# Long convolution and soft mixture of experts on one core: combine weights gathered per batch in SBUF instead of written per tile

## The chip, the core and the metric

One core of a Trainium2 chip runs the whole program in one launch. The metric is the device time in microseconds. The engines named below are TensorE (PE, with its weight loads PEld), VectorE (DVE), ScalarE (ACT), GpSimd (POOL) and SyncE (SP), which here only issues DMAs.

## The reference

A causal convolution of each of 8 sequences (5696 positions, 128 channels) with one filter of full length, then a soft mixture of experts over all 45568 tokens:

```python
Xf = np.fft.rfft(x, n=2*S, axis=1); Hf = np.fft.rfft(h, n=2*S, axis=0)
x = np.fft.irfft(Xf * Hf[None], n=2*S, axis=1)[:, :S, :].reshape(B*S, D)
logits = x @ phi                            # 45568 x 32 slots (8 experts x 4)
d = softmax(logits, over all tokens)        # dispatch weights
slot_input = d.T @ x                        # 32 x 128
slot_out[e] = relu(slot_input[e] @ w1[e]) @ w2[e]
c = softmax(logits, over the 32 slots)      # combine weights
out = c @ slot_out
```

The output needs `slot_out`, which needs every token. The combine weights `c` (45568 x 32 numbers) therefore have to be kept from the time a token tile is made until the last stage.

## The kernel before

**Stages.** The convolution is two transform stages forward (`first_stage`, then `stage_b1` with the product in frequency), and two back (`stage_b2`, then `stage_c1`). Between them stand two internal DRAM tensors, `f` and `z`. The rest works on 32 token tiles, T = 0 to 31, four for each of 8 batches (`NQ = 4`). For a tile, `load_pair` brings 1.4 MB of `z` (five DMAs, of 64, 8, 8, 8 and 2 rows of 16 KB), and then:

- `stage_c1` multiplies back to tokens: 16 matmuls, and folds on DVE, ACT and POOL into the buffer `y`. It runs `stage_c4` of an earlier tile between its two halves.
- `stage_c2` transposes `y` (PE, copies `yt` on ACT), `stage_c3` makes logits `lt`, `column_max` keeps the running maximum (DVE).
- `stage_c4` transposes the logits into `L` (tokens x slots), takes `exp` into `dt` (ACT), clears the last rows of `dt` (POOL, line 439), and subtracts the row maximum of `L` (DVE, POOL line 447). `stage_c5` transposes `dt` into `d` (PE line 454). `softmax` finishes `L`, which then holds the combine weights.
- `dispatch` adds `d.T @ y` to the accumulator `acc`.
- `stage_c6` transposes `L` so that slots lie on partitions (4 transposes, line 502).

**Where the combine weights go.** The last stage reads one table, `cT`, of 128 x 8 x 89 x 16 (slots and quarters on partitions; batch, row, column). It takes 45.6 KB of each partition, and there is room for it only when the transform tables have been freed, near the end. Until then `stage_c6` copies its PSUM bank in one ACT instruction into a staging tile `cst` (line 512) and stores 180 KB of it to the DRAM tensor `c_t` (line 513). That is done for T = 0 to 24. From T = 25 on `cT` exists, and `stage_c6` writes its four quarters straight into it (line 507; `place` gives the reversed or forward rows and columns of each quarter). In the last loop `fetch_c` and `load_c` bring the stored tiles back, a batch at a time (720 KB, line 518) into two buffers `cl`; `placed_c` and `place_all` copy them into `cT`, two copies on POOL and two on ACT for each batch (line 524), and then fetch again.

**Order.** The program gives every engine its instructions in the order in which the code is written; nothing moves them later. The main loop runs steps t = 0 to 80, two steps to a tile, with the order of the work in a step given by the strings `ORDER_E` and `ORDER_O` (line 577). All DMAs but four at the start are issued by SP, in program order. They share 8 completion semaphores in turn, so that each DMA waits until the eighth one before it has landed.

**The end.** The main loop ends at t = 80 (lines 625 to 641) with T = 26 as `V`. Then the tables are freed, `cT` is allocated (line 667), and a last loop (lines 699 to 734) runs V = 27 to 31. Its order for V = 28 and later is: `stage_c2(V)`, `dispatch(V-1)`, `stage_c6(V-2)`, `stage_c3(V)`, `column_max(V)`, `placed_c`, `stage_c1(V+2)` with `stage_c4(V)` inside it, `placed_c`, `stage_c5(V)`, `softmax(V)`, and for V = 28 and 29 half of the load of `w2s`. `stage_c1(30)` is so in the iteration V = 28, and `stage_c1(31)` in V = 29. The data of tile 30 are loaded in iteration 27, after `stage_c1(28)` has read the buffer `zd`, and those of tile 31 after `stage_c1(29)` has read `zc`. After the loop come the experts (lines 741 to 797) and the output matmuls with `cT` (lines 812 to 839), which write 23 MB.

Of the kernel before, what the change touches and what calls it, by code (L numbers as in the profile page):

```python
# [10 lines left out]
F32 = mybir.dt.float32  # L11
AF = mybir.ActivationFunctionType
# [65 lines left out]
def kernel(  # L78
# [24 lines left out]
    nc = tc.nc  # L103
    P = 128
    B, S, D = x.shape
# [4 lines left out]
    N1, N2 = 90, 64  # L110
    R1, HALF, NP = S // N2, N2 // 2, N1 // 2
    CH = 4
    NJ = HALF // CH
# [16 lines left out]
        for n, t in zip(("s1", "i1", "w", "v", "turn"), transform_tables(S, N1, N2, CH, X0))]  # L130
    fd = [nc.dram_tensor(f"f_{g}", (NP, 2, N2, 2, D), F32, kind="Internal").ap() for g in range(B + 1)]
    zd = [nc.dram_tensor(f"z_{b}", (NP, 2 * N2, 2, D), F32, kind="Internal").ap() for b in range(B)]
    cd = nc.dram_tensor("c_t", (P, B * NQ, Q, 2, MH), F32, kind="Internal").ap()

    const = ctx.enter_context(tc.tile_pool(name="const", bufs=1))
    ident = const.tile([P, P], F32, name="ident")
# [347 lines left out]
                                           scalar=scales.pop(T)[:, 0:1], in1=ap_[:, 0:D + 1],  # L484
                                           op0=AL.mult, op1=AL.add)

    kept, tail = [], {}

    def place(T, n, k):

        b, j = 2 * T // NJ, 2 * T % NJ
        v, f = divmod(k, 2)
        rows = slice(MH, R1) if v else slice(MH - 1, None, -1)
        e_ = 2 * NJ - 1 - j
        cols = slice(e_, e_ - 2 * n, -1) if f else slice(j, j + 2 * n)
        return tail["cT"][:, b, rows, cols].rearrange("p r (n h) -> p r n h", h=2)

    def stage_c6(T):
        L = Ls.pop(T)
        p = bank()  # L500
        for k in range(Q):
            nc.tensor.transpose(p[:, k * TR:(k + 1) * TR],
                                L[0:TR, k, :, :].rearrange("p i s -> p (i s)"), ident[0:TR, 0:TR])
        pv = of_tokens(p)
        if tail:
            for k in range(Q):
                nc.scalar.activation(place(T, 1, k)[:, :, 0, :],
                                     pv[:, k, :, 0:MH - k // 2].rearrange("p h r -> p r h"), AF.Copy)
            return
        kept.append(T)  # L510
        st = cpool.tile([P, Q, 2, MH], F32, name="cst", tag="cst", bufs=1)
        nc.scalar.activation(st[:, :, :, :], pv, AF.Copy)
        nc.sync.dma_start(out=cd[:, T, :, :, :].rearrange("p k h r -> p (k h r)"),
                          in_=st[:, :, :, :].rearrange("p k h r -> p (k h r)"))

    def load_c(T, n):
        st = tail["pool"].tile([P, NQ, Q, 2, MH], F32, name="cl", tag="cl")
        nc.sync.dma_start(out=st[:, 0:n, :, :, :].rearrange("p n k h r -> p (n k h r)"),
                          in_=cd[:, T:T + n, :, :, :].rearrange("p n k h r -> p (n k h r)"))
        return st  # L520

    def place_all(T, n, st):
        for k in range(Q):
            (nc.gpsimd.tensor_copy if k < 2 else nc.scalar.copy)(
                out=place(T, n, k),
                in_=st[:, 0:n, k, :, 0:MH - k // 2].rearrange("p n h r -> p r n h"))

    def join_quarters():

# [49 lines left out]
    for t in range(last_front + 1):  # L579
        us = list(units(t))  # L580

        def pair(lag):
            T, half = divmod(t - LAG_C - lag, 2)
            return T if half == 0 and 0 <= T < NT else None

        def prefetch(last):
            nonlocal loaded
            while loaded < len(queue) and queue[loaded][1] <= last:
                load_g(queue[loaded][0])
                loaded += 1  # L590

        def slot_b():
            fresh = bool(us)
            if fresh:
                u = us.pop(0)
                stage_b1(u, t < LAG_C or t >= NA)
                wait_b2.append(u)
            if len(wait_b2) > fresh:
                stage_b2(wait_b2.pop(0))

        T, U = pair(0), pair(2)
        after = []
        work_ = {
            "z": lambda: load_pair(pair(-1)) if pair(-1) is not None else None,
            "x": lambda: load_x(t + XAHEAD) if t < NA else None,
            "p": lambda: prefetch(t + 1) if t % NJ else None,
            "P": lambda: prefetch(t + 2),
            "q": lambda: prefetch(t + 1),
            "X": lambda: first_low(t) if t < NA else None,
            "Y": lambda: first_high(t) if t < NA and t % 2 else None,  # L610
            "f": lambda: [fold(t + 1, comp) for comp in range(2)] if t < NA else None,
            "d": lambda: dispatch(pair(3)) if pair(3) is not None else None,
            "b": lambda: slot_b(),
            "1": lambda: after.append(stage_c1(T, lambda: stage_c4(U) if U is not None else None))
            if T is not None else stage_c4(U) if U is not None else None,
            "w": lambda: [a_() for a_ in after],
            "2": lambda: stage_c2(pair(1)) if pair(1) is not None else None,
            "6": lambda: stage_c6(pair(5)) if pair(5) is not None else None,
            "5": lambda: stage_c5(U) if U is not None else None,
            "3": lambda: stage_c3(pair(1)) if pair(1) is not None else None,  # L620
            "m": lambda: column_max(pair(1)) if pair(1) is not None else None,
            "s": lambda: softmax(U) if U is not None else None,
            "g": lambda: prefetch(t + 1) if t % NJ == 0 else None,
        }
        if t == last_front:
            if pair(-1) is not None:
                load_pair(pair(-1))
            assert T is None and U is None
            if pair(3) is not None:
                dispatch(pair(3))  # L630
            slot_b()
            slot_b()
            slot_b()
            stage_c2(pair(1))
            slot_b()
            assert not us and not wait_b2
            V = pair(1)
            stage_c6(V - 2)
            stage_c3(V)
            column_max(V)  # L640
            break
        for c_ in (ORDER_E if t % 2 else ORDER_O):
            work_[c_]()
        assert not us
        if t == NA:
            lead.close()
            wts = inner.enter_context(tc.tile_pool(name="wts", bufs=1, side="right"))
            w1s = wts.tile([P, E, F], F32, name="w1s")
        if NA < t <= NA + E:
            nc.sync.dma_start(out=w1s[:, t - NA - 1, :], in_=moe_w1[t - NA - 1])  # L650
# [14 lines left out]
    load_pair(V + 2)  # L665
    nc.sync.dma_start(out=w1s[:, E - 1, :], in_=moe_w1[E - 1])
    tail["cT"] = last.tile([P, B, R1, 2 * NJ], F32, name="cT")
    w2s = last.tile([P, E, NFC, D], F32, name="w2s")
    tail["rep4"] = rep4 = last.tile([P, Q, NSL], F32, name="rep4")
    tail["pool"] = cload.enter_context(tc.tile_pool(name="cload", bufs=2))  # L670
    y_ = tail["pool"].tile([P, Q * CH, D + 1], F32, name="y2", tag="y2", bufs=1)

    after = stage_c1(T, lambda: stage_c4(V))
# [6 lines left out]
        nc.gpsimd.tensor_copy(out=rep4[r, :, :],  # L680
                              in_=ident[r, r].unsqueeze(1).broadcast_to([NSL, Q, NSL]))
    load_pair(T + 2)
    landed = []

    def fetch_c():
        if kept:
            n = min(NQ, len(kept))
            landed.append((kept[0], n, load_c(kept[0], n)))
            del kept[0:n]

    def placed_c():
        if landed:
            place_all(*landed.pop(0))
            fetch_c()

    fetch_c()
    fetch_c()
    assert (B - 1) * NQ == T + 1
    for V in range(T, NT):
        if V > T:  # L700
            stage_c2(V)
        dispatch(V - 1)
        stage_c6(V - 2)
        if V == T:
            stage_c2(V)
        stage_c3(V)
        column_max(V)
        if V > T:
            placed_c()
        N = T + 1 if V == T else V + 2  # L710
        after = None
        if N < NT:
            after = stage_c1(N, lambda: stage_c4(V))
            load_pair(N + 2)
        else:
            stage_c4(V)
        if after:
            after()
        if V > T:
            placed_c()  # L720
        stage_c5(V)
        if V == NT - 1:
            join_quarters()
            dispatch(V)
        softmax(V)
        if V == T:
            ybufs.insert(0, y_)
            stage_c1(T + 2, lambda: None)()
            load_pair(T + 4)
        else:  # L730
            for i in range(4 * (V - T - 1), min(4 * (V - T), E), 2):
                nc.sync.dma_start(
                    out=w2s[:, i:i + 2, :, :],
                    in_=moe_w2[i:i + 2].rearrange("e (p c) d -> p e c d", p=P))
    stage_c6(NT - 2)
    assert list(Ls) == [NT - 1] and not (ys or ds or prods or gs or zs or xs or folded or wait_b2
                or kept or landed)


    cload.close()  # L740
# [128 lines left out]
```

## Time and profile before

| | |
|---|---|
| device time, median of 3 runs | 871.62 us (869.36 to 871.84) |
| profiled execution, device time | 869.17 us |
| span of its instructions | 867.4 us |
| mean granted TensorE clock | 0.954 |
| PE busy, share of the span | 89% |
| DVE, ACT, POOL busy | 71%, 51%, 47% |
| moved by DMA | 272.46 MB, mean 314 GB/s |

Times inside the run are microseconds from the first instruction. The stages that matter here are: the main loop in its steady state (about 230 to 630 us, some 20 us for a tile), its end (630 to 722), the last loop (722 to 785), the experts (785 to 802) and the output (802 to 867). A wait is charged to what released it last; idle time of an engine matters only where something on the chain to the end waits for it.

### The profile page before, as it was taken

The page shows a single profiled execution, that of the slowest core. Times are in us where ns is not written, and L with a number is a line of the kernel's source. Part 1 is how long each engine was busy: PE and PEld are TensorE (multiplying, and loading weights), DVE is VectorE, ACT ScalarE, POOL GpSimd, SP SyncE. Part 2 cuts the span into 40 slices and gives each one's busy share as a digit, 9 for nine tenths or more (in the row PEclk, how much of TensorE's full clock was granted, in tenths as well). Part 3 has the DMA queues.
Part 4 walks back from the last instruction along what each step waited for, and adds up shares of the span by engine and source line. Part 5 has one row for each costly group of instructions (what it writes and reads, how often), then busy time and mean ns, then how long its engine had stood idle before and what let it go on. Part 6 is the DMA issues. An engine that isn't in the chain of part 4 may idle for free.

```text
span 867.4 us, 20489 instructions
## 1 busy us (share of the span) xinstructions
PE 770.7 (89%) x7796; PEld 376.2 (43%) x7796; DVE 619.2 (71%) x928; ACT 441.6 (51%) x904; POOL 403.7 (47%) x385
## 2 busy tenths in 40 slices
PE   5888888888999999999999999999988879977893
PEld 1122333234444444444444444444444444444882
DVE  3059967667777878877888788877789995953552
ACT  2433344344555565556566556655544445773541
POOL 4453433245565555656555655556434432671000
PEclk9999999999999999999999999999999898989865
DMA  9899899999999999999999999999998986580898
GB/s 294 272 296 310 296 333 342 332 332 334 339 315 321 340 324 329 347 329 345 338 339 337 338 338 339 346 327 343 320 314 283 320 301 247 219 305 2 335 405 341
DMA packets 156109, 272.46 MB, mean 314 GB/s; under 512 B 12183, under 2 KB 113687, under 8 KB 152870
## 3 DMA queue, kind: packets, MB, share of 16 engines
q1 hardware_dynamic: 155435, 270.85, 90.2%
q8 instruction: 62, 1.02, 0.5%
q10 hardware_dynamic: 576, 0.31, 0.1%
q14 instruction: 36, 0.29, 0.1%
HBM read 142.81 MB, written 128.21 MB: 312 GB/s over the span
## 4 chain that ended last, share of the span: by engine, by line
PE 60%; DMA 15%; DVE 11%; SPq 3%; issue 2%; POOL 1%; ACT 1%; DVEq 0%; ACTq 0%
PE bank L217 14%; PE bank L365 13%; PE bank L309 7%; PE bt L267 7%; PE bank L393 6%; DMA zc<-z 6%; DMA out_dram<-o 3%; PE bank L478 3%; DVE yf L294 2%; DVE p L285 2%; DVE bt L285 2%; SPq L346 2%; DMA gt<-f 2%; PE op L822 2%; PE bank L402 2%
## 5 line engine op out<-in xcount | busy, mean ns | idle before, releaser
L206 POOL TENSOR_TENSOR x<-xc 128x512 f32<-128x512 f32 x144 | 180.0, 1274 | 229.5 <-PE bank L217 208.6
L217 PE MATMUL bank<-x,s 128*32 128x512 f32 (+1 forms) x1152 | 227.7, 613 | 16.0 <-DMA xc<-in_h_dram 8.1
L315 ACT ACTIVATE zst<-bank 128x512 f32<-128x512 f32 (+1 forms) x184 | 98.6, 586 | 190.9 <-PE bank L309 173.9
L220 ACT ACTIVATE fst<-bank 128x512 f32<-128x512 f32 x216 | 127.4, 598 | 109.5 <-PE bank L217 93.5
L285 DVE TENSOR_TENSOR p<-bt,Hi 128x1024 f32<-128x1024 f32 x96 | 111.4, 1160 | 33.7 <-PE bt L267 32.8
L309 PE MATMUL bank<-yf,vt 64*64 64x256 f32 x1440 | 103.1, 392 | 27.5 <-DVE yf L294 27.5
L365 PE MATMUL bank<-zc,i 128*64 128x512 f32 x480 | 115.8, 604 | 12.1 <-DMA zc<-z 8.2
L217 PEld LDWEIGHTS bank<-x,s 128*32 128x32 f32 (+1 forms) x1152 | 56.1, 124 | 155.5 <-issue 76.2
L294 DVE TENSOR_TENSOR yf<-bt,p 128x512 f32<-128x512 f32 x192 | 119.4, 663 | 3.3
L267 PE MATMUL bt<-gt,wt 64*64 64x256 f32 x1620 | 113.7, 388 | 5.8 <-DVE Hi L289 2.4
L285 DVE TENSOR_TENSOR bt<-bt,Hr 128x1024 f32<-128x1024 f32 x96 | 113.0, 1177 | 0.0
L267 PEld LDWEIGHTS bt<-gt,wt 64*64 64x64 f32 x1620 | 54.0, 132 | 80.6 <-issue 36.7
L309 PEld LDWEIGHTS bank<-yf,vt 64*64 64x64 f32 x1440 | 57.2, 136 | 58.9 <-issue 27.8
L384 POOL TENSOR_TENSOR y<-y,op 128x512 f32<-128x512 f32 x64 | 77.9, 1217 | 8.3 <-DVE op L370 5.2
L370 DVE TENSOR_TENSOR y<-bank,y 128x512 f32<-128x512 f32 x32 | 22.1, 691 | 72.8 <-PE bank L365 72.6
L393 PE MATMUL bank<-ident,y 109*128 109x109 f32 x512 | 64.3, 278 | 0.7 <-DVE y L384 0.7
L384 POOL TENSOR_TENSOR y<-y,om 128x512 f32<-128x512 f32 x54 | 64.0, 1185 | 2.1
L365 PEld LDWEIGHTS bank<-zc,i 128*64 128x64 f32 x480 | 30.5, 136 | 74.8 <-issue 47.1
L393 PEld LDWEIGHTS bank<-ident,y 109*128 109x128 f32 x512 | 54.3, 151 | 16.7 <-issue 11.1
L395 ACT ACTIVATE yt<-bank 128x360 f32<-128x360 f32 x128 | 51.4, 492 | 3.1 <-PE bank L393 3.1
L439 POOL MEMSET dt<- 64x8 f32 x32 | 3.4, 106 | 104.8 <-issue 70.7
L822 PE MATMUL op<-so,cT 32*128 32x128 f32 x704 | 45.6, 368 | 4.7 <-ACT o L831 4.3
(97 smaller groups left out, 824.6 us busy)
## 6 DMA issues: line engine op xcount, KB each, us to landing
gt<-f SPq DMA_DIRECT2D x99, 512.0 KB
z<-zst SPq DMA_DIRECT2D x88, 512.0 KB
f<-fst SPq DMA_DIRECT2D x144, 240.0 KB
zc<-z SPq DMA_DIRECT2D x30, 1024.0 KB
xc<-in_x_dram SPq DMA_DIRECT2D x64, 320.0 KB
f<-fst SPq DMA_DIRECT2D x144, 120.0 KB
out_dram<-o SPq DMA_DIRECT2D x16, 1024.0 KB
zc<-z SPq DMA_DIRECT2D x90, 128.0 KB
```

What stands on the lines that cost most here:

```text
L206: nc.gpsimd.tensor_tensor(out=y_[:, :, :], in0=t_[:, 0, :, :], in1=t_[:, 1, ::-1, :], op=AL.subtract if comp else AL.add)
L217: nc.tensor.matmul(p[o * width:(o + 1) * width, :], s1[:, comp + G, k], folded[(c, comp)][:, :, :].rearrange("p n d -> p (n d)"), start=Tr ...
L220: nc.scalar.activation(st[:, :, G, :], p[:, :].rearrange("p (n d) -> p n d", d=D), AF.Copy)
L267: nc.tensor.matmul(bt[q * HP:(q + 1) * HP, a, o, :], wt[r, 2 * i + q, :], t_[r, 2 * o + q, :, :].rearrange("p c d -> p (c d)"), start=True ...
L285: nc.vector.tensor_tensor(out=p_, in0=pv, in1=h_, op=AL.mult)
L294: eng.tensor_tensor(out=y_[r, 0:k, c, :], in0=pv[:, :, c, :], in1=pi[r, 0:k, 1 - c, :], op=op_)
L309: nc.tensor.matmul(bz[q][a * HP:(a + 1) * HP, o * 2 * D:(o + 1) * 2 * D], vt[r, i, a, :], y_[r, a * m + o, :, :].rearrange("p c d -> p (c ...
L315: nc.scalar.activation(st[:, 0:m, q, :], bz[q][:, 0:m * 2 * D].rearrange("p (o x) -> p o x", o=m), AF.Copy)
L365: nc.tensor.matmul(p[h_ * HP:(h_ + 1) * HP, :], i1[0:kr, tab, :], t_[0:kr, h_, o, :, q, :], start=True, stop=True)
L384: eng.tensor_tensor(out=part_, in0=part(v, 0), in1=o_[:, :, :], op=sign)
L393: nc.tensor.transpose(p[:, i * TR:(i + 1) * TR], ys[T][0:TR, k * CH + i, 0:D], ident[0:TR, 0:TR])
L822: nc.tensor.matmul(pq[q][:, k * D:(k + 1) * D], cT[rows, b, r0:r0 + RW, :] if k < n else cL[rows, :, :], so4[rows, :], start=True, stop=True)
```

## The change

A tile `cbatch` in SBUF (128 x 89 x 16, 5.7 KB of each partition) has the layout that one batch has in `cT`. `stage_c6` now always writes its four quarters with four ACT copies: into `cbatch` while `cT` doesn't exist, into `cT` after that. After the fourth tile of a batch, `cbatch` is stored with one DMA of 712 KB, six times in all (batches 0 to 5). `stage_c6(24)`, the first tile of batch 6, moves from before `stage_c3(26)` to after the allocation of `cT`, and so writes to `cT`. In the last loop there is no fetching and placing any more: behind `load_pair(T + 2)`, which is tile 29, six DMAs load batches 0 to 5 from DRAM straight into `cT`. The buffers `cl` and the functions `load_c`, `place_all`, `fetch_c` and `placed_c` are gone.

```diff
-    cd = nc.dram_tensor("c_t", (P, B * NQ, Q, 2, MH), F32, kind="Internal").ap()
+    cd = nc.dram_tensor("c_t", (B - 1, P, R1, N2 // 4), F32, kind="Internal").ap()
...
-    kept, tail = [], {}
-    def place(T, n, k):
+    tail = {}
+    cbatch = ypool.tile([P, R1, 2 * NJ], F32, name="cbatch")
+    def place(T, k):
...
-        cols = slice(e_, e_ - 2 * n, -1) if f else slice(j, j + 2 * n)
-        return tail["cT"][:, b, rows, cols].rearrange("p r (n h) -> p r n h", h=2)
+        cols = slice(e_, e_ - 2, -1) if f else slice(j, j + 2)
+        home = tail["cT"][:, b, :, :] if tail else cbatch
+        return home[:, rows, cols]
...
-        if tail:
-            for k in range(Q):
-                nc.scalar.activation(place(T, 1, k)[:, :, 0, :],
-                                     pv[:, k, :, 0:MH - k // 2].rearrange("p h r -> p r h"), AF.Copy)
-            return
-        kept.append(T)
-        st = cpool.tile([P, Q, 2, MH], F32, name="cst", tag="cst", bufs=1)
-        nc.scalar.activation(st[:, :, :, :], pv, AF.Copy)
-        nc.sync.dma_start(out=cd[:, T, :, :, :].rearrange("p k h r -> p (k h r)"),
-                          in_=st[:, :, :, :].rearrange("p k h r -> p (k h r)"))
-    def load_c(T, n):
...
-    def place_all(T, n, st):
         for k in range(Q):
-            (nc.gpsimd.tensor_copy if k < 2 else nc.scalar.copy)(
-                out=place(T, n, k),
-                in_=st[:, 0:n, k, :, 0:MH - k // 2].rearrange("p n h r -> p r n h"))
+            nc.scalar.activation(place(T, k),
+                                 pv[:, k, :, 0:MH - k // 2].rearrange("p h r -> p r h"), AF.Copy)
+        b, last_of = divmod(T, NQ)
+        if not tail and last_of == NQ - 1:
+            nc.sync.dma_start(out=cd[b].rearrange("p r j -> p (r j)"),
+                              in_=cbatch[:, :, :].rearrange("p r j -> p (r j)"))
...
             V = pair(1)
-            stage_c6(V - 2)
+            assert (V - 2) % NQ == 0
             stage_c3(V)
...
     tail["cT"] = last.tile([P, B, R1, 2 * NJ], F32, name="cT")
+    stage_c6(V - 2)
...
     load_pair(T + 2)
-    landed = []
...
-    fetch_c()
-    fetch_c()
+    for b in range(B - 2):
+        nc.sync.dma_start(out=tail["cT"][:, b, :, :].rearrange("p r j -> p (r j)"),
+                          in_=cd[b].rearrange("p r j -> p (r j)"))
...
-        if V > T:
-            placed_c()
...
-        if V > T:
-            placed_c()
```

More of the change, by code (lines that the diff above doesn't have):

```diff
@@ L504, in stage_c6 @@
         pv = of_tokens(p)
-        if tail:
-            for k in range(Q):
-                nc.scalar.activation(place(T, 1, k)[:, :, 0, :],
-                                     pv[:, k, :, 0:MH - k // 2].rearrange("p h r -> p r h"), AF.Copy)
-            return
-        kept.append(T)
-        st = cpool.tile([P, Q, 2, MH], F32, name="cst", tag="cst", bufs=1)
-        nc.scalar.activation(st[:, :, :, :], pv, AF.Copy)
-        nc.sync.dma_start(out=cd[:, T, :, :, :].rearrange("p k h r -> p (k h r)"),
-                          in_=st[:, :, :, :].rearrange("p k h r -> p (k h r)"))
-    def load_c(T, n):
[L517 to L520, printed above, removed]
-    def place_all(T, n, st):
-        for k in range(Q):
-            (nc.gpsimd.tensor_copy if k < 2 else nc.scalar.copy)(
-                out=place(T, n, k),
-                in_=st[:, 0:n, k, :, 0:MH - k // 2].rearrange("p n h r -> p r n h"))
+        for k in range(Q):
+            nc.scalar.activation(place(T, k),
[4 more added lines that the diff above has]
+                              in_=cbatch[:, :, :].rearrange("p r j -> p (r j)"))
     def join_quarters():
@@ L667 @@
     tail["cT"] = last.tile([P, B, R1, 2 * NJ], F32, name="cT")
+    stage_c6(V - 2)
     w2s = last.tile([P, E, NFC, D], F32, name="w2s")
     tail["rep4"] = rep4 = last.tile([P, Q, NSL], F32, name="rep4")
-    tail["pool"] = cload.enter_context(tc.tile_pool(name="cload", bufs=2))
+    tail["pool"] = cload.enter_context(tc.tile_pool(name="cload", bufs=1))
     y_ = tail["pool"].tile([P, Q * CH, D + 1], F32, name="y2", tag="y2", bufs=1)
@@ L682 @@
     load_pair(T + 2)
-    landed = []
[L685 to L693, printed above, removed]
-            fetch_c()
-    fetch_c()
-    fetch_c()
+    for b in range(B - 2):
+        nc.sync.dma_start(out=tail["cT"][:, b, :, :].rearrange("p r j -> p (r j)"),
+                          in_=cd[b].rearrange("p r j -> p (r j)"))
     assert (B - 1) * NQ == T + 1
@@ L735 @@
     stage_c6(NT - 2)
-    assert list(Ls) == [NT - 1] and not (ys or ds or prods or gs or zs or xs or folded or wait_b2
-                or kept or landed)
+    assert list(Ls) == [NT - 1] and not (ys or ds or prods or gs or zs or xs or folded or wait_b2)
     cload.close()
```

## The prediction

> **What bounds the kernel now.** I read the page first, then stretches, then the last loop on PE, POOL and SP in order of time. The stretches (columns: length; busy us of PE, PEld, DVE, ACT, POOL; clock; DMA share; GB/s):
>
> ```profile
> 228.00:630.00 402.00, 395.08 (x4056) 183.78 (x4054) 318.53 (x493) 235.20 (x487) 229.53 (x213) 1.00 0.97 334
> 746.00:765.00 19.00, 16.81 (x136) 8.45 (x134) 18.42 (x30) 14.61 (x34) 15.70 (x16) 1.00 0.51 176
> 765.00:785.00 20.00, 12.07 (x121) 8.49 (x121) 8.86 (x20) 14.06 (x36) 11.62 (x16) 0.83 0.66 258
> ```
>
> In the main loop PE idles 7 us of 402 and the DMA engines are 97% busy: both bind, and ACT (59%) and POOL (57%) have room. In the last loop nothing is full. POOL and ACT are busy there with the copies into `cT`; the group rows and the longest PE waits from 715 to 803 us:
>
> ```profile
> L512 ACT ACTIVATE cst<-bank 128x360 f32<-128x360 f32 x25 | 13.1, 522 | 0.3 <-PE bank L502 0.3
> L524 POOL COPY cT<-cl 128x360 f32<-128x360 f32 (+1 forms) x14 | 11.7, 868 | 2.5 <-DMA cl<-c_t 2.5
> L524 ACT COPY cT<-cl 128x352 f32<-128x352 f32 (+1 forms) x14 | 10.5, 799 | 3.6 <-DMA cl<-c_t 3.6
> L507 ACT ACTIVATE cT<-bank 128x90 f32<-128x90 f32 (+1 forms) x28 | 4.6, 266 | 5.9 <-PE bank L502 5.9
> PE bank L454 <- POOL dt L439: 6.6, 4, 3.8
> ```
>
> PE waits for the POOL memset of `dt`. The chain shows what holds it in V = 30: a `cl` load, and copies behind it.
>
> ```profile
> 760.74 1.69 POOL cT L524 x2
> 762.43 0.02 issue
> 762.45 8.72 DMA cl<-c_t
> ...
> 772.11 0.84 POOL cT L524
> ```
>
> Next, what SP issues before `stage_c1(30)`, and the PE row of that stage:
>
> ```profile
> 728.32 3.68 SPq L346 DMA_DIRECT2D zc<-z  x5
> 732.05 0.89 SPq L518 DMA_DIRECT2D cl<-c_t  x2
> 738.69 3.15 SPq L346 DMA_DIRECT2D zd<-z  x5
> 742.86 3.12 SPq L346 DMA_DIRECT2D zc<-z  x5
> 747.01 1.94 PE L365 MATMUL bank<-zd,i 96*64 96x512 f32 x8
> 757.76 1.94 PE L365 MATMUL bank<-zc,i 128*64 128x512 f32 x8
> ```
>
> The landing times are in the trace's records of the DMA semaphores (the last update before the semaphore is used again):
>
> ```
> load                 first issue   last piece landed   read by PE from
> tile 29 (zc)         728.32        738.39              739.17
> cl, batch 0          732.05        740.20
> cl, batch 1          732.49        741.97
> tile 30 (zd)         738.69        746.90              747.01
> tile 31 (zc)         742.86        752.27              757.76
> ```
>
> Tile 30 lands 0.11 us before PE reads it, and directly behind the two `cl` loads. That is the place to watch.
>
> **What the Trainium skill says.** "DMA: Bandwidth & Descriptors", section "Queues, rings and completion order": on each DMA engine descriptors are consumed in ring order, so loads issued ahead on the same queue go first. The landings agree: `cl` 0, `cl` 1, tile 30, one behind the other. "TensorE: Matmul & The Clock Gate", section "Part 1: The HAM clock gate", says that after about 3.4 us of idling PE runs at half clock until it has been busy for such a window. The trace agrees: PE idles from 770.35 to 774.11, and the 16 matmuls of line 393 then take 3.11 us instead of 1.66.
>
> **The change, part by part.** Times are for the profiled span of 867.4 us (device 869.17); the median is 2.45 us above that run, and I add the difference found to the median.
>
> 1. *Main loop, ACT.* 24 tiles have four copies of 0.266 us (row L507) in place of one of 0.522 us: +0.54 us of ACT for a tile of 20 us, in the gap between the last `yt` copy and `stage_b2`. PE does 2.9 us of `dispatch`, `stage_b1` and `stage_b2` before ACT or the PSUM bank is needed again. Cost 0; uncovered it would be 13 us.
>
> 2. *Main loop, DMA.* 24 stores of 180 KB become 6 of 712 KB, nearly the same bytes (4.4 MB). At 334 GB/s a store takes 0.55 us, the big one 2.2. SP is 8 to 10 us behind the compute here, and `zc` lands only 0.1 to 1.2 us before it is read in most tiles, so this isn't free: three tiles of a batch gain up to 0.55 us where they wait now, and one has a burst of 1.6 us net. Slack at the loads behind the first five bursts (tiles 7, 11, 15, 19, 23) is 0.09, 0.09, 0.34, 0.65, 0.35 us. Bounds: +6.3 us if each burst stalls by 1.6 less its slack and nothing is regained; -2.5 if the lighter tiles take back the waits at tiles 5, 6, 10, 21, 22 and the bursts are absorbed. The work of the queue over a batch is unchanged, so I take 0.
>
> 3. *Wait for `cbatch`.* The first tile of the next batch must wait until the store has been read out. The single stores land 6.3 to 8.8 us after issue, and the next copy comes 2.7 to 7 us after that; 1.6 us more still fits. Cost 0. Uncovered, `zst` and `lt` would queue behind it on ACT, and PE behind their banks.
>
> 4. *`stage_c6(24)` moves.* Its four transposes (0.59 us) stood in the shadow of the last `yt` copy and now stand ahead of `stage_c1(27)`: +0.6 us. In step 6 that disappears in a longer wait.
>
> 5. *Copies gone from the last loop.* 14 POOL and 14 ACT copies, 22.2 us busy, and the waits for `cl`. Without them I rebuild the iterations from PE rows. A full one with `stage_c1`: 4.4 us for the stage with `stage_c4` inside, 0.65 for `stage_c5`, 1.65 for line 393, 1.1 for line 478, 0.6 for 502, 0.8 for 402: 9.1 us from one `stage_c1` to the next (now 10.75). From `stage_c1(31)` to the last line 454 (784.20 now): 5.0 to `stage_c2(30)`, then twice 7.05 with the wait for lt, L, `dt` and its memset, and 0.55 for the transposes: 19.65 us (now 26.4). Gain 1.6 + 6.8 = 8.4 us, if the data are there.
>
> 6. *Six loads ahead of tile 30.* They stand behind tile 29 and before tiles 30 and 31 in the queue, where two stood. Their semaphores come free between 731.4 and 737.1, so all six are in the queue before tile 30 is issued at 738.7. The two `cl` loads took 1.81 and 1.77 us of it; four more take 7.0. Tile 30 lands at 746.9 + 7.0 = 753.9, tile 31 at 759.3. PE arrives at `stage_c1(30)` at 747.6 and waits 6.3 us. That isn't all: a window of 3.4 us is idle, so the clock halves. It stays so for 3.0 to 6.4 us of work, 4.7 in the middle, which loses 2.35 us. The wait holds everything: `stage_c4(28)` is inside `stage_c1(30)`, and ACT, DVE and POOL have their next work from there.
>
> Sum: 753.9 + 2.35 + 9.1 + 19.65 = 785.0 against 784.20: +0.8 us. In V = 30 and 31 PE then idles 2.25 us within 2.9 us twice, and idle gaps of 1.8 to 2.7 us in the trace (634.76, 670.13) were followed by a half-clock window, up to 1.7 us each: I add 1.5. Together +2.3 us. Experts and output (784.9 to 867) keep their length: `w2s` lands at about 769 instead of 779.5, and is needed at 797.
>
> **Forecast.** 871.6 + 2.3 = 873.9 us: the copies go, and the wait that they hid behind takes their place. Chance 0.62. Its own range: 870 to 878.
>
> **Rival, faster.** The queue lets tile 30 through in time, because the loads are quicker or start earlier than I think. Then 747.6 + 9.1 + 19.65 = 776.4, -7.8 us, with perhaps 1 lost to the clock: about 864.5. It decides where tile 30 lands before some 751.5 (784.2 less 28.75, less the 3.9 for the clock). For it: DMA idles from 755.5 to 760 now, so there is room in the queue overall, and 8.4 us of gain are real. Against it: the order on SP, and the rate of 1.77 us a load that the same bytes already show at this place. Chance 0.18.
>
> **Rival, much slower.** The bursts in the main loop find no slack: +6.3 us from part 2, and +2.3: 880. For it: DMA at 97% and slacks of 0.09 us. Against it: the tiles between bursts get lighter by the same sum. Chance 0.20.
>
> **How the numbers follow.** A difference of about 0.3% (2.6 us) is what can be told from none here. The forecast, at +2.3 with some 2.2 either way, gives slower 0.28, same 0.33, faster 0.01. The faster rival gives 0.15 and same 0.03; the slower one 0.20. Sums: faster 0.16, same 0.36, slower 0.48. The range leaves out the faster rival's centre and the upper end of the slower one: 868.5 to 879.
>
> **What would show it.** Right: PE idle for 5 to 7 us before line 365 on `zd` in V = 28, released by the DMA of tile 30; a half-clock window from about 753; no wait over 2 us for the memset afterwards; some 785 at the last line 454. In the main loop: ACT without waits at `cbatch`, PE idle still 5 to 10 us of 402. Wrong: tile 30 landed by 750 (faster), or PE idle of 1 us or more behind each batch's store (slower), or ACT waiting for the store of `cbatch`.

## The result and the profile after

| | before | after |
|---|---|---|
| device time, median of 20 runs each | 872.04 us | 875.87 us |
| profiled execution: span, mean clock | 867.4 us, 0.954 | 875.6 us, 0.94 |

The ratio is 1.005, 95% interval 1.0032 to 1.0067: slower by 3.8 us in the medians, where 2.3 was forecast. The stretches of the changed kernel (columns as in the prediction: length; busy us of PE, PEld, DVE, ACT, POOL; clock; DMA share; GB/s):

```profile
228.00:630.00 402.00, 396.66 (x4076) 184.26 (x4076) 320.20 (x496) 240.51 (x551) 230.77 (x215) 1.00 0.97 335
746.00:765.00 19.00, 14.58 (x96) 7.48 (x92) 12.27 (x18) 6.59 (x18) 7.13 (x7) 0.64 0.91 368
765.00:785.00 20.00, 17.38 (x182) 11.41 (x175) 12.89 (x29) 11.48 (x31) 8.16 (x9) 0.83 0.02 9
```

The main loop is what it was: PE idles 5.3 us of 402 (6.9 before). From 746 on DMA is now 91% busy (51% before) and then empty, POOL's 15.7 us have become 7.1, and the clock is 0.64 where it was 1.00. The order in which SP issues (start, length, what) shows how that comes about:

```profile
729.11 3.14 SPq L346 DMA_DIRECT2D zc<-z  x5
732.29 3.71 SPq L672 DMA_DIRECT2D cT<-c_t  x6
740.09 3.14 SPq L346 DMA_DIRECT2D zd<-z  x5
```

PE waits for the last of these. Its rows in order of time (start, time to the end of the group, what; in brackets the idle time before it and what ended it):

```profile
752.62 3.68 PE L365 MATMUL bank<-zd,i 96*64 96x512 f32 x8 [4.15 <-DMA zd<-z]
...
766.93 1.94 PE L365 MATMUL bank<-zc,i 128*64 128x512 f32 x8
...
778.97 1.12 PE L454 MATMUL bank<-ident,dt 128*128 128x128 f32 x4 [1.96 <-POOL dt L439]
```

Tile 29 landed at 736.85, tile 30 at 752.43. PE waits 4.15 us, and then the same eight matmuls of line 365 take 3.68 us instead of 1.94: the throttle records show half clock from 750.72 to 764.37. `stage_c1(31)` follows 14.31 us later.

Cut at the same landmarks, the two profiled executions compare so:

| stretch | before | after | difference |
|---|---|---|---|
| start to `stage_c1(4)` | 258.26 | 259.30 | +1.0 |
| `stage_c1(4)` to `stage_c1(26)` | 441.56 | 439.44 | -2.1 |
| `stage_c1(26)` to `stage_c1(27)` | 23.45 | 23.97 | +0.5 |
| `stage_c1(27)` to the first output matmul | 79.08 | 84.41 | +5.3 |
| first output matmul to the end | 65.03 | 68.51 | +3.5 |

Not all of the +5.3 us is tile 30's. From `stage_c1(26)` to `stage_c1(28)`, before a tile waits behind the six loads, the changed kernel took 36.9 us instead of 34.4. In both kernels PE waits over 3 us for `yf` at the end of the main loop, and half clock comes with it; it lasted from 715.27 to 722.10 before, and from 713.17 to 726.82 now, so that the first matmuls of `stage_c1(27)` fall into it. Before, then now:

```profile
723.27 1.94 PE L365 MATMUL bank<-zc,i 128*64 128x512 f32 x8
```

```profile
720.43 1.43 PE L402 MATMUL bank<-yt,phi 128*32 128x360 f32 x8 [0.56 <-ACT yt L395]
721.79 0.99 PE L504 MATMUL bank<-ident,L 109*128 109x109 f32 x4
722.71 3.68 PE L365 MATMUL bank<-zc,i 128*64 128x512 f32 x8
```

The 0.56 us of idle time is where the transposes of `stage_c6(24)` stood before; they now follow line 402.

The last row of the table was not foreseen. In its middle both kernels are bound by DMA. Two stretches of 20 us, of the kernel before and of the changed one:

```profile
818.00:838.00 20.00, 18.82 (x254) 17.34 (x251) 10.54 (x18) 9.08 (x18) 0.00 (x0) 0.67 1.05 405
```

```profile
823.00:843.00 20.00, 18.68 (x230) 17.35 (x231) 9.50 (x16) 8.05 (x16) 0.00 (x0) 0.50 1.04 381
```

DMA is full in both (the share adds up the time of the packets, so it can pass 1), and yet it moves 381 GB/s instead of 405. The trace has the time of each packet: the 11392 packets of 2048 bytes that carry `o` to DRAM took 84.5 ns each before and 89.5 after. Their code is the same. What differs is where `o` lies: the tile `cbatch` (5696 bytes of each partition) came and `cst` (1440) went, so that all that is allocated later moved by 4256 bytes, and `o` with it, from byte 172288, a multiple of 256, to 176544, which leaves 160. (The step follows from the two sizes; the two addresses are those of the layout and stand in no view of the profile.)

Of the variants below, `e4_busy_pe`, `e9_after_256` and `e13_last_mm` had an execution more than 1.5% above their fastest in front of the profiler, so that of these profiles only rows, rates and packet times are used.

### The profile page after: what moved, and what is told of

It reads as the page before. It is cut to its first block, busy times and chain, and to the rows that moved or that the text cites. A ratio compares the mean times of both kernels' runs of the same rounds, so it can differ in the third digit from the quotient of the medians.

```text
span 875.6 us, 20491 instructions
## 1 busy us (share of the span) xinstructions
PE 777.0 (89%) x7796; PEld 378.6 (43%) x7796; DVE 617.6 (71%) x928; ACT 437.0 (50%) x965; POOL 392.1 (45%) x371
## 4 chain that ended last, share of the span: by engine, by line
PE 55%; DMA 20%; DVE 10%; issue 5%; SPq 3%; ACT 1%; POOL 1%; DVEq 0%; POOLq 0%; ACTq 0%
PE bank L365 13%; PE bank L217 12%; PE bank L309 7%; PE bt L267 7%; PE bank L393 6%; DMA xc<-in_x_dram 6%; DMA out_dram<-o 5%; DMA zc<-z 4%; DMA gt<-f 3%; PE bank L478 3%; DVE yf L294 2%; PE bank L402 2%; PE bank L431 2%; DVE p L285 2%; DVE bt L285 2%
## 5 line engine op out<-in xcount | busy, mean ns | idle before, releaser
L365 PE MATMUL bank<-zc,i 128*64 128x512 f32 x480 | 119.1, 618 | 13.4 <-DMA zc<-z 8.7
L309 PE MATMUL bank<-yf,vt 64*64 64x256 f32 x1440 | 101.0, 387 | 25.1 <-DVE yf L294 24.8
L384 POOL TENSOR_TENSOR y<-y,op 128x512 f32<-128x512 f32 x64 | 77.5, 1211 | 11.6 <-DVE op L370 8.3
L793 PE MATMUL op<-so,cT 32*128 32x128 f32 x704 | 48.6, 391 | 4.2 <-ACT o L802 3.8
```

The costliest lines, as they stand in the source:

```text
L309: nc.tensor.matmul(bz[q][a * HP:(a + 1) * HP, o * 2 * D:(o + 1) * 2 * D], vt[r, i, a, :], y_[r, a * m + o, :, :].rearrange("p c d -> p (c ...
L365: nc.tensor.matmul(p[h_ * HP:(h_ + 1) * HP, :], i1[0:kr, tab, :], t_[0:kr, h_, o, :, q, :], start=True, stop=True)
L384: eng.tensor_tensor(out=part_, in0=part(v, 0), in1=o_[:, :, :], op=sign)
```

## The experiments

Two questions were open: what the wait for tile 30 really costs, with its clock, and whether the place of `o` makes the output stage longer. All kernels below are the changed one with the edit shown, unless it says otherwise. Ratios are against the kernel before on the same chip. Where the table has no length of a stage, it isn't used.

| run | median us | ratio (95% interval) | `stage_c1(27)` to output | output stage | `o` packet ns |
|---|---|---|---|---|---|
| e1_loads_last | 872.31 | 1.0003 (0.9979 to 1.0028) | 72.75 | 68.47 | 89.3 |
| e2_two_ahead | 870.14 | 0.9984 (0.9962 to 1.0005) | 77.54 | 68.43 | 89.3 |
| e3_four_ahead | 872.85 | 1.0004 (0.9979 to 1.0028) | 72.64 | 68.54 | 89.4 |
| e4_busy_pe | 875.29 | 1.0033 (1.0011 to 1.0054) | | | 89.3 |
| e5_two_stores | 881.75 | 1.0113 (1.0073 to 1.0153) | 77.62 | 68.44 | 89.4 |
| e7_last_256 | 869.06 | 0.9971 (0.9950 to 0.9992) | 76.38 | 65.93 | 84.6 |
| e8_before_shift | 873.19 | 1.0005 (0.9979 to 1.0030) | 76.92 | 68.22 | 89.3 |
| e9_after_256 | 873.90 | 1.0001 (0.9982 to 1.0021) | | | 84.6 |
| e10_busy_mm | 881.78 | 1.0126 (1.0084 to 1.0168) | 87.69 | 68.58 | 89.4 |
| e11_last_64 | (one run, 867.34) | | 72.61 | 68.65 | 89.4 |
| e12_four_mm | 874.23 | 1.0029 (1.0003 to 1.0055) | 79.77 | 68.39 | 89.4 |
| e13_last_mm | 861.37 | 0.9872 (0.9830 to 0.9914) | | | 84.5 |

### The loads at other places in the queue

Two stay where they are and four go behind tiles 30 and 31 (e2_two_ahead); e3_four_ahead has 4 in place of the 2, and e1_loads_last has all six behind the tiles.

```diff
     load_pair(T + 2)
-    for b in range(B - 2):
+    for b in range(2):
...
             load_pair(T + 4)
+            for b in range(2, B - 2):
+                nc.sync.dma_start(out=tail["cT"][:, b, :, :].rearrange("p r j -> p (r j)"),
+                                  in_=cd[b].rearrange("p r j -> p (r j)"))
```

> The changed kernel with the six loads of cT issued behind the loads of tiles 30 and 31 instead of ahead of them. Theory (the six loads hold up tile 30, and the wait halves the PE clock): PE finds tile 30 in place at about 748 us, no half-clock window follows, about 20 us from stage_c1(31) to the last line 454; some 8 us faster than before the change, about 864 (ratio 0.990 to 0.993). Rival (the bursts of the batch stores in the main loop cost what the change lost): the last loop gets shorter but the main loop stays 4 us or more longer than before, ratio 0.995 to 1.00.

> The changed kernel with two of the six loads ahead of tile 30, as many as before the change, and four behind tile 31. Theory (1.77 us of queue for each load ahead): tile 30 lands 7 us earlier than with six ahead, PE waits less than 1 us for it, within 1 us of the kernel with none ahead: about 865. Rival (it is the number of loads in all or the main loop): close to the changed kernel, 873 to 876.

> The changed kernel with four of the six loads ahead of tile 30 and two behind tile 31. Theory: tile 30 lands 3.5 us earlier than with six ahead, PE waits 0.5 to 2 us, perhaps one half-clock window: 866 to 870, between the kernels with two and with six. If the wait alone decided, without the clock, the times with 2, 4 and 6 ahead would lie on a line with 1.77 us a load; with the clock the step from 4 to 6 is the larger one.

From `stage_c1(27)`, tile 30 landed after 23.9 us with none of the loads ahead, 24.9 with two, 25.6 with four, and 29.7 with six. PE starts on it after 24.9, 25.7, 25.7 and 29.9 us: it waits for the tile not at all with none or two ahead, 0.9 us with four and 4.15 with six. Tile 30 can't be issued before `stage_c1(28)` has read its buffer, which leaves the first loads time to drain; the last two delay it by 4 us. With the tile in time the clock stays whole in this stretch (e1_loads_last; it was 0.64):

```profile
746.00:765.00 19.00, 17.63 (x168) 9.11 (x164) 18.17 (x32) 11.30 (x31) 8.80 (x10) 1.00 0.93 360
```

So taking away the cause takes away the loss of this loop: 72.6 to 77.5 us to the first output matmul instead of 84.4, and in device time 4 to 6 us (ratios of 0.9984 to 1.0004, where the change has 1.0050). But 864 to 870 us had been expected, and no ratio falls below 1 by more than its interval: the output stage stayed at 68.4 to 68.5 us in all three. One thing more shows in the profiles: from `stage_c1(31)` to the first output matmul e1_loads_last, e3_four_ahead and e11_last_64 took 37.6 us, e2_two_ahead, e7_last_256 and e5_two_stores 41.2 to 41.6, with the same instructions between. The long ones have 13.7 us of half clock there, the short ones 3.4.

### The place of `o`

One line, here of e7_last_256 (on e1_loads_last) and of e9_after_256 (on the change), with which `o` leaves no remainder of 256:

```diff
     cL = last.tile([P, B, 2 * NJ], F32, name="cL")
+    last.tile([P, 24], F32, name="pad")
```

With 40 in place of 24 it is e8_before_shift, on the kernel before (remainder 160), and with 8 e11_last_64, on e1_loads_last (remainder 192).

> The variant with the six table loads behind tiles 30 and 31 (e1_loads_last), plus 96 unused bytes in front of the output tile `o`, which then starts on a multiple of 256 bytes of a partition (remainder 160 in the change, 0 in the kernel before). Theory A (the output stage is longer because each 2048-byte packet reads a row that no longer starts on a multiple of 256): packets back to 84.5 ns from 89.3, output stage 65.0 us instead of 68.5, time 3.4 us under e1_loads_last's, about 869 against a before of 872, ratio near 0.996. Theory B (the output stage is longer for another reason, such as more half-clock time there or the earlier end of the last loop): packets and stage stay at 89 ns and 68.5 us, ratio 1.000.

> The kernel before with 160 unused bytes in front of `o`, so that it starts with the remainder 160 as in the change; nothing else differs. Theory A (place of `o`): packets 89 ns, output stage 68.5 us instead of 65.0, time +3.4 us, ratio 1.004. Theory B: no difference, ratio 1.000, output stage 65.0 us.

> The change itself with 96 unused bytes in front of `o` (remainder 0). Theory A: output stage 65.0 us, and with it the whole difference of the change goes: 875.5 - 3.4 = 872.1, ratio 1.000; the last loop keeps its wait for tile 30 and its half clock. Theory B: 68.5 us and a ratio of 1.004.

> e1_loads_last with 32 unused bytes in front of `o`: it starts on a multiple of 64 that is not one of 256 (remainder 192). If only multiples of 256 give packets of 84.5 ns, they stay at 89 and the output stage at 68.5 us. If 64 is enough, packets are back to 84.5 ns and the stage to 65.0 to 66.

Twenty microseconds of the output stage, of e8_before_shift, then of e7_last_256:

```profile
817.00:837.00 20.00, 17.16 (x232) 16.03 (x225) 9.50 (x16) 8.04 (x16) 0.00 (x0) 0.58 1.04 380
```

```profile
817.00:837.00 20.00, 19.21 (x241) 17.35 (x237) 10.27 (x18) 8.80 (x18) 0.00 (x0) 0.59 1.05 404
```

The rate goes with the place, both ways: 380 in the kernel before once `o` is moved, 404 in the variant once it is moved back; at the same clock of 0.58 and 0.59, so half clock isn't the reason. (Over the whole stage e3_four_ahead had 52.4 us of half clock and took 68.5 us, e7_last_256 had 54.7 and took 65.9.) In all fourteen profiles the packets took 84.5 or 84.6 ns where `o` leaves no remainder, and 89.3 to 89.5 elsewhere. A multiple of 64 that isn't one of 256 doesn't help (e11_last_64: 89.4 ns). The Trainium skill says why that can be ("DMA: Bandwidth & Descriptors", section "How a descriptor splits into AXI transactions"): a transaction (a single transfer on the bus, of up to 256 bytes) starts on a multiple of 256 bytes, so a piece that doesn't start there needs one more. For 2048 bytes with remainder 160 that makes, by an estimate from this rule, 9 transactions instead of 8, or 69 beats of 32 bytes instead of 64. The direction and the boundary agree with the runs; the packets took 5.7 to 5.9% longer, less than either estimate.

In the device time, e9_after_256 is at 1.0001 where the change was at 1.0050: 4.3 us less, with some 2 us either way, where 3.4 was expected. That can be the whole measured loss, but needn't be: its median, 873.90 us, still lies 1.45 us above that of the kernel before on the same chip, 872.45. e7_last_256 is 0.0032 under e1_loads_last, 2.8 us, with intervals of some 2 us each way. For e8_before_shift the stage grew by 3.2 us in the profile, but its ratio of 1.0005 doesn't show that: 1.004 lies just outside its interval. That miss stays open.

### The idle time before `stage_c1(30)`, filled

With transposes (e4_busy_pe):

```diff
         if N < NT:
+            if V == T + 1:
+                for _ in range(6):
+                    p = bank()
+                    for i in range(CH):
+                        nc.tensor.transpose(p[:, i * P:(i + 1) * P], ident[:, :], ident[:, :])
```

With matmuls (e12_four_mm; e10_busy_mm has 14 of them):

```diff
         if N < NT:
+            if V == T + 1:
+                for _ in range(4):
+                    p = bank()
+                    nc.tensor.matmul(p[:, :], ident[:, :], w1s[:, 0, 0:512],
+                                     start=True, stop=True)
```

> The changed kernel as it is, with 24 transposes of the identity (some 4 us of PE, results unused) ahead of stage_c1(30), where PE waits. Theory (more than half of the loss is the half clock after the wait): PE still starts stage_c1(30) when tile 30 lands, at about 752.5, but at full clock, and stage_c1(31) comes 9 to 10 us later instead of 14.3; 4 to 5 us faster than the changed kernel, about 871, no slower than before the change. Rival (the wait itself is the loss and the clock is hidden by other engines): no faster than the changed kernel, 875 to 877.

> The change with 14 unused matmuls (w1s as the moving operand, 512 columns) on PE just before stage_c1(30), where it idles for tile 30; in e4_busy_pe 24 transposes stood in their place and half clock came all the same. Theory A (the clock falls because PE has too few matmuls in a window, and transposes don't count for it): half clock doesn't come at 750 or is one window shorter, stage_c1(30) to stage_c1(31) takes 9.5 to 11 us instead of 14.3, time 3 to 5 us less than the change, ratio 0.998 to 1.000. Theory B (the loss of 14.3 against 9.1 us isn't the idle time's: loads of the table and of tile 31 hold the stage, or half clock comes from the power of the stretch before): the stage stays at 13.5 us or more and the ratio at 1.003 to 1.005.

> As e10_busy_mm, with 4 matmuls in place of 14 (each took 0.88 us there, 12.3 in all, and PE was busy with them for 8 us after tile 30 had landed; the four take 3.5 us of an idle time of 4.15). Theory A (too few matmuls in a window halve the clock; they alone hold it): no half clock between 745 and 768, stage_c1(30) to stage_c1(31) 8.7 to 9.5 us, first output matmul 79 to 80 us after stage_c1(27) instead of 84.4, time about 5 us under the change: 870 to 871, ratio 0.998. Theory B (in e10_busy_mm it was the late start of stage_c1(30), with all loads landed, that made the stage short): 13.5 us and more from stage_c1(30) to stage_c1(31), ratio 1.003 to 1.005.

PE in e4_busy_pe:

```profile
755.25 2.40 PE L691 MATMUL bank<-ident 128*128 128x128 f32 x20
758.19 0.66 PE L691 MATMUL bank<-ident 128*128 128x128 f32 x4 [0.54 <-DVE acc L483]
760.04 2.81 PE L365 MATMUL bank<-zd,i 96*64 96x512 f32 x8 [1.19 <-DMA zd<-z]
...
773.61 1.94 PE L365 MATMUL bank<-zc,i 128*64 128x512 f32 x8
```

PE in e12_four_mm:

```profile
744.34 3.70 PE L690 MATMUL bank<-w1s,ident 128*128 128x512 f32 x8
748.50 1.94 PE L365 MATMUL bank<-zd,i 96*64 96x512 f32 x8 [0.46 <-DMA zd<-z]
...
757.19 1.94 PE L365 MATMUL bank<-zc,i 128*64 128x512 f32 x8
```

The transposes kept PE busy for 3.1 us, and half clock came all the same (760.96 to 771.20), with 13.57 us to `stage_c1(31)`; the ratio is 1.0033, where no loss against the kernel before was expected. Four matmuls, in the records eight passes of 0.43 us, fill the same wait: no half clock from 722.5 to 770.3, and 8.69 us. Tile 30 came no earlier in relation to `stage_c1(27)` (29.4 us, 29.7 in the change). So of the 14.3 us, 5.6 are the clock's, in this pair of profiles. The Trainium skill has the difference ("TensorE: Matmul & The Clock Gate", section "Part 4: PE-mode transpose"): a transpose doesn't count as PE being busy in the same way. These runs agree, but e4_busy_pe also left 1.3 us more idle time than e12_four_mm, so they don't separate the two completely.

e10_busy_mm was mis-sized: each of its 14 matmuls took 0.88 us (two passes), 12.3 in all where the wait has 4.15, so PE was still at them 8.0 us after tile 30 had landed. The stage took 8.70 us, with the clock whole, but began too late, and the ratio of 1.0126 is the highest of all.

The 5 us that e12_four_mm wins in the profile (79.77 after 84.41) are 2 us in the ratio (1.0029 after 1.0050), with intervals that overlap; 0.998 was expected. What the half clock after the wait costs is thus shown inside the stage, and not in the device time.

### The burst of the store, doubled

On e1_loads_last:

```diff
             nc.sync.dma_start(out=cd[b].rearrange("p r j -> p (r j)"),
                               in_=cbatch[:, :, :].rearrange("p r j -> p (r j)"))
+            nc.sync.dma_start(out=cx[b].rearrange("p r j -> p (r j)"),
+                              in_=cbatch[:, :, :].rearrange("p r j -> p (r j)"))
```

> e1_loads_last with each of the six batch stores done twice (the second into a table of its own), so that each burst in the main loop is 1.42 MB, 4.3 us at the rate of 334 GB/s, instead of 2.1. Theory A (the slack between tiles absorbs a burst of 2 us, as the prediction took it, and the bursts of the change cost nothing): PE's idle time from 228 to 630 rises from 5.6 us to at most 9, stage_c1(4) to stage_c1(26) by under 4 us, ratio to before 1.000 to 1.005. Theory B (PE and DMA bind together, so that each byte of a burst is paid): +2.1 us for each of the six, 11 to 13 us in all, ratio 1.013 to 1.015; the change would then pay up to 6 us for its own bursts.

The main loop of e1_loads_last, then of e5_two_stores:

```profile
228.00:630.00 402.00, 396.39 (x4068) 183.84 (x4067) 318.69 (x494) 239.39 (x547) 231.04 (x214) 1.00 0.97 333
```

```profile
228.00:630.00 402.00, 391.62 (x4018) 181.53 (x4018) 315.59 (x487) 236.56 (x543) 228.09 (x212) 1.00 0.97 336
```

PE's idle time goes from 5.6 to 10.4 us; `stage_c1(4)` to `stage_c1(26)` takes 449.1 us instead of 441.4, and the ratio rises by 0.011, 9.6 us. That is nearer to theory B: of some 13 us for six more stores (2.1 each at 334 GB/s), 8 to 10 are paid. The queue has little left. What the change adds is less than that, for its stores carry the bytes that 24 small ones carried before: its loop, 439.4 us, is no longer than the one before (441.6), and the seven other variants whose spans are used and whose main loop is the same took 436.3 to 441.4.

### A version from the findings

e7_last_256 with matmuls where PE waits for the memset of `dt`:

```diff
         else:
             stage_c4(V)
+            for _ in range(NT - V):
+                p = bank()
+                nc.tensor.matmul(p[:, :], ident[:, :], w1s[:, 0, 0:512],
+                                 start=True, stop=True)
```

> e7_last_256 (six loads behind tile 31, `o` on a multiple of 256) with two unused matmuls of 0.88 us before stage_c5(30) and one before stage_c5(31), where PE waits 2.4 and 1.5 us for the memset of dt. The same loop took 37.6 us from stage_c1(31) to the first output matmul in two runs and 41.2 and 41.6 in two others; the long ones show more half clock there. Theory A (a window with too few matmuls halves the clock[...]): with the matmuls the short course comes each time, 35 to 38 us, output stage 65.0 to 66, time about 2 us under e7_last_256: near 867, ratio 0.9945 to 0.997. Theory B (the matmuls only take PE time away, the clock falls all the same): 39 to 42 us, ratio 0.997 to 1.000.

PE in e13_last_mm (the same place in e1_loads_last has the idle times 2.43 and 1.53 before line 454):

```profile
776.59 1.88 PE L690 MATMUL bank<-w1s,ident 128*128 128x512 f32 x4
779.18 0.66 PE L454 MATMUL bank<-ident,dt 128*128 128x128 f32 x4 [0.70 <-POOL dt L439]
...
784.77 1.02 PE L690 MATMUL bank<-w1s,ident 128*128 128x512 f32 x2
786.47 0.66 PE L454 MATMUL bank<-ident,dt 128*128 128x128 f32 x4 [0.67 <-POOL dt L439]
```

The matmuls lie wholly in the waits, and the clock is whole from 734.5 to 792.5. The ratio is 0.9872 (0.983 to 0.9914): this beats both kernels, the one before by 11 us. That is more than its theory gave (about 2 us under e7_last_256; it is 8.6 under, on another chip). Where the other 6 us come from was not shown, and the ratio rests on six executions. Nor does the profile show that the matmuls won anything: it is of the slowest of the six (872.11 us; the others took 857.6 to 866.2), its way from `stage_c1(31)` to the first output matmul took 38.3 us, where theory A has 35 to 38 and three variants without these matmuls took 37.6, and half clock came later instead, from 792.54 to 795.96.

## Why the prediction was right, and where it was not

The direction and nearly the size were right, and the mechanism named, a wait for tile 30 behind the six loads with half clock after it, was at work. But three terms were too small in the profiles, by 1.9, 3.3 and 3.5 us. The total came close only because the profiled executions lie further apart (+8.25) than the medians (+3.8), and that is luck.

- **Parts 1 and 3, ACT and the wait for `cbatch`.** Held. The copies took 0.328 us, more than the 0.266 assumed. PE waited for ACT 1.0 us in all between 228 and 640 (0.7 before), and the group row of the changed kernel shows no idle time of ACT before the copies:

```profile
L508 ACT ACTIVATE cbatch<-bank 128x90 f32<-128x90 f32 (+1 forms) x96 | 17.3, 328 | 0.0
```

- **Part 2, the stores.** Held at 0. e5_two_stores shows that this was no wide margin: more bytes would have been paid. The much slower rival had the right weak place and the wrong amount.
- **Part 4, `stage_c6(24)`.** Too small: +0.6 predicted, and +0.5 from `stage_c1(26)` to `stage_c1(27)`, but +2.5 up to `stage_c1(28)`, with the longer half clock. In the nine profiles of the change and its variants whose spans are used this way took 36.5 to 38.0 us, in the two of the kernel before (e8_before_shift is the second) 34.4 and 35.0. Nor did it disappear in a longer wait, as forecast: tile 30 is issued only after `stage_c1(28)`, at 740.09 instead of 738.69. No run moved `stage_c6(24)` back, so that its cause is argued and not shown.
- **Part 5, the copies gone.** Nearly held. 9.1 us predicted from `stage_c1(30)` to `stage_c1(31)`; with the clock whole it was 8.7 where PE had waited for tile 30 before (e10_busy_mm, e12_four_mm), and 10.3 in the six variants whose tile came in time, with waits of 0.6 us for the memset of `dt` and 0.5 for `yt` (9.3 in e3_four_ahead); 19.65 us from `stage_c1(31)` to the last line 454, 20.1 in e1_loads_last and e3_four_ahead, 22.06 in the change, where 1.5 us had been added for the clock.
- **Part 6, six loads.** Tile 30 predicted at 753.9, seen at 752.43; PE waits 4.15 us for it, where 6.3 was predicted (5 to 7 as a sign of being right), and the last line 454 starts at 788.99 instead of 785. Between the two kernels the 1.77 us a load held (15.6 us after tile 29 instead of 8.5, for four more loads), but it is no law: the runs with none, two and four ahead differ by 1.7 us altogether. The mis-sized term is the half clock after the wait: 4.7 us of it, losing 2.35, was predicted; it stayed 13.65 us and lost 5.6. The prediction took from the Trainium skill ("TensorE: Matmul & The Clock Gate", section "Part 1: The HAM clock gate") that one busy window brings the clock back; this run does not show that: PE was busy from 752.62, and the clock came back at 764.37, 11.75 us later.
- **"Experts and output keep their length."** The experts did (18.15 and 18.13 us from the last line 454 to the first output matmul). The output didn't: +3.5 us, because a new tile moved a later one off a multiple of 256. The step that failed is this one; the diff was read for instructions and not for addresses.
- **The faster rival.** Its course, tile 30 in time, was made in e1_loads_last and e3_four_ahead: the last loop is then up to 6.4 us shorter than before, of 7.8 forecast. It still gives 872 and not 864.5, for the output stage takes half of that back, and 1.5 us go between `stage_c1(26)` and `stage_c1(27)`; with `o` in place as well it gives 869.

Not settled: how the 3.8 us of the medians divide. In the ratio, taking the loads away gave back 4 to 6 us, the place of `o` 4.3 and the filled wait 1.8. These need not add up to 3.8, for what the missing copies gain stands against them, but each has 2 us and more either way, and the same last loop differs by 5 us between executions.

## What to carry to other kernels

When a tile is added or dropped, look at the addresses of all that is allocated behind it: a DMA-bound stage that the change doesn't touch lost 6% of its rate here. A load that is put ahead of another in a queue costs little while the second is waiting for its buffer anyway (here two cost no wait and four 0.9 us), and its length after that; so count what the queue can drain before the release. One wait of PE cost more in clock (5.6 us) than in time (4.15) here. Unused matmuls in it kept the clock whole in that stage; what they are worth in device time was not shown beyond the noise.

## What the runs showed that was not expected

- Packets of 2048 bytes from a row that starts on a multiple of 256 took 84.5 ns, with remainders of 160 or 192 89.3 to 89.5; the stage then ran at 380 instead of 404 GB/s.
- One wait of 4.15 us halved the clock for 13.65 us, four windows of 3.41, though PE was busy from 752.62 to its end; what in that work kept it halved was not shown.
- The half clock in the stretch with two waits of 2.4 and 1.5 us came to 3.4 us in some executions and to 13.7 in others of the same instructions.
- A matmul of 512 columns stands in the records as two passes, which start 0.43 us apart at whole clock. The matmuls of line 365 (`zd`), whose results fill half of the rows, start two at a time: four of them took 1.94 us, four of `w1s`, which fill all rows, 3.70. The mean of a row's length by its count (0.24 us) is therefore not the time of one matmul.
